# The end of a load stream: the last weight in three pieces, and a small load moved between them

## The chip, the cores and the metric

The kernel runs on one core of one Trainium2 chip. Times are device microseconds of that core, over several executions; the "span" is the part of an execution that the profile covers, from the first to the last instruction, and it is 1.8 to 2.1 us shorter than the time (that difference will matter). Ratios are the mean time of one kernel's fast runs over that of the kernel before in the same rounds, with a 95% interval, so they are not quite the ratio of the medians quoted beside them. A run is called slow when it lies over 1.5% above the fastest one of the same kernel, and fast otherwise; a single run has no known state.

## The reference, cut to what matters

One decode step of a transformer block: layer norm, attention of 8 batches with one query row over a window of 1024 cached keys, an FFN with a gate, and `x + s * g` at the end.

```python
x = A_x                                  # 8 x 1 x 512, bf16
xn = layernorm(x)
s = attention(xn, k_cache[:, :, -1024:], v_cache[:, :, -1024:], wq) @ wo   # wo: 4096 x 512
g = silu((gelu(xn @ w_gate) * (xn @ w_up)) @ w_down)                       # F = 1792
return x + s * g
```

Nearly all of the work is reading: 32 MiB of keys and values, 4 MiB each of wq and wo, 5.25 MiB of FFN weights, 47.46 MB in all (an MB is a million bytes here, an MiB 2^20).

## The kernel before

Every large load is issued by SyncE on one queue, in the order of use; the last things that it brings are `wd` (w_down) and the two halves of `wo`. The second half comes in two pieces, 12 and 4 rows of each partition. After the last piece only its matmuls, two VectorE operations and the output DMA remain. `x` is loaded twice at the very start on ScalarE's queue: as `x_sb` for the layer norm, and as `xr`, laid out for the residual at the end.

```python
nc.scalar.dma_start(out=x_sb, in_=x_flat)
xr = consts.tile([P, NW], BF16, name="xr")
nc.vector.memset(xr, 0.0)
nc.scalar.dma_start(out=xr[0:P:4, :], in_=x_flat.rearrange("b (q n) -> q b n", n=NW))

def load_rows(src, rows, r0, n, name):
    t = ring.tile([P, n, src.shape[1]], BF16, name=name, tag="slot")
    nc.sync.dma_start(out=t, in_=src.rearrange("(p r) n -> p r n", r=rows)[:, r0 : r0 + n, :])
    return t
# ... wq, then per unit the keys and values, with their matmuls (cut) ...
wd_t = load_rows(B_w_down, FJ, 0, FJ, "wd_t")
wo_t = [[load_rows(A_wo[: HT * Dh, :], WI, 0, WI, "wo_t")]]
LAST = 4
wo_t.append([
    load_rows(A_wo[HT * Dh :, :], WI, 0, WI - LAST, "wo_t"),
    load_rows(A_wo[HT * Dh :, :], WI, WI - LAST, LAST, "wo_t"),
])
# ... the FFN, and oR, the attention output laid out for wo (cut) ...
for t in range(NT):                       # the two halves of wo
    i = 0
    for w in wo_t[t]:                     # the pieces
        for r in range(w.shape[1]):       # rows: 16 in a half
            for q in range(NQ):           # 4 matmuls a row
                nc.tensor.matmul(s_ps[32*q : 32*(q+1), :], oR[:, t, i, :],
                                 w[:, r, q*NW : (q+1)*NW], ..., tile_position=(0, 32*q))
            i += 1
nc.vector.tensor_tensor(out=tmp, in0=s_ps, in1=g_sb, op=ALU.mult)
nc.vector.tensor_tensor(out=out_sb, in0=tmp, in1=xr, op=ALU.add)
nc.sync.dma_start(out=..., in_=out_sb[0:P:4, :])
```

The softmax here doesn't subtract the row's maximum and nothing guards it: scores larger than these inputs give would overflow.

## Time and profile before

| | before |
|---|---|
| time, median of 3 | 122.81 us (122.78 to 122.95) |
| span of the profiled run | 121.1 us |
| read from memory | 47.46 MB |
| share of the chain that ended last on DMA | 84% |
| last wo piece landed | 116.75 us |

First the page of the kernel before: the busy tenths of TensorE and of the DMA engines in 40 slices of the span, the granted TensorE clock in tenths, the bytes moved, and the queues (q1 is SyncE's, q10 ScalarE's, q8 brings instructions).

```profile
PE   0000799696877977979679684999969798754660
PEclk9999999999999999999999996579999955555555
DMA  4999999999999999999999999999999999999710
GB/s 100 428 435 431 411 427 419 430 422 427 419 425 425 425 425 419 427 422 425 419 430 417 433 417 430 427 419 425 422 436 438 417 417 445 428 428 415 290 68 3
q1 hardware_dynamic: 5796, 47.46, 93.3%
q8 instruction: 16, 0.26, 0.8%
q10 hardware_dynamic: 52, 0.02, 0.1%
```

The stream runs without a gap from the second slice to the 37th, at 411 to 445 GB/s, and TensorE is busy for 70% of the span. So the kernel ends when the stream ends, plus the little that follows. (The chain also has 12% of TensorE, at 74 to 87 us, since the issue of a wo load waits there for a slot that TensorE frees; loads issued earlier kept the DMA engines busy meanwhile.) Note the clock: TensorE has half of its clock in the last eight slices.

The timeline of the last stretch (start, length, engine, line, operation, tile, count; in brackets the idle time before it and what ended that) shows what follows.

```profile
111.96 1.90 PE L357 MATMUL s_ps<-wo_t,oR 128*32 128x128 bf16 x64 [1.19 <-DMA wo_t<-in_A_wo_dram]
115.60 1.90 PE L357 MATMUL s_ps<-wo_t,oR 128*32 128x128 bf16 x64 [1.74 <-DMA wo_t<-in_A_wo_dram]
117.55 0.29 DVE L365 TENSOR_TENSOR tmp<-s_ps,g_sb 128x128 f32<-128x128 f32 x1 [5.93 <-PE s_ps L357]
117.87 0.29 DVE L367 TENSOR_TENSOR out_sb<-tmp,xr 128x128 bf16<-128x128 f32 x1
118.19 0.69 SPq L368 DMA_DIRECT2D out_dram<-out_sb  x1
```

The second half of wo waits for its 12-row piece, which lands at 115.56, and then runs its 64 matmuls without another wait: when it reaches the 4-row piece, that has landed too. In the windows of the same stretch (after the engines' busy times come the clock, the DMA share, and GB/s) the DMA engines do not stop together:

```profile
113.00:113.50 0.50, 0.50 (x31) 0.50 (x24) 0.00 (x0) 0.00 (x0) 0.00 (x0) 0.50 0.91 352
113.50:114.00 0.50, 0.36 (x16) 0.17 (x5) 0.00 (x0) 0.00 (x0) 0.00 (x0) 0.50 0.54 229
114.00:115.00 1.00, 0.00 (x0) 0.00 (x0) 0.00 (x0) 0.00 (x0) 0.00 (x0) 0.50 0.45 188
115.00:116.00 1.00, 0.40 (x17) 0.40 (x20) 0.00 (x0) 0.00 (x0) 0.00 (x0) 0.50 0.43 176
116.00:116.50 0.50, 0.50 (x31) 0.50 (x24) 0.00 (x0) 0.00 (x0) 0.00 (x0) 0.50 0.13 49
```

From 113.5 to 116 us only about half of them work. The trace also records sixteen increments of a load's semaphore; for the 12-row piece the last one came at 115.56, and TensorE, which waited for that load, started at 115.60. For the last piece (4 rows) the sixteen came at

```
113.62 113.68 113.72 113.76 113.77 113.77 113.82 | 114.61 | 115.08 | 116.38 116.47 116.48 116.52 116.53 116.55 116.75
```

The increments go with engines that fall quiet: after the first seven, from 113.85 to 114.60 us, the DMA share is 0.55, or nine of the 16 engines, and 16, 9, 8 and 7 packets are under way at 113.0, 113.9, 114.7 and 115.2 us. So seven engines are done about 2.8 us before the last seven (mean against mean). TensorE did not start on the 12-row piece before its last increment, so the last seven set the kernel's end.

### The profile page before, as it was taken

What the parts mean: (1) busy time and instruction counts of PE and PEld (TensorE: products, weight loads), DVE (VectorE), ACT (ScalarE), POOL (GpSimd) and SP (SyncE); (2) the same over time, 40 slices, a digit from 0 to 9 for tenths busy, and PEclk for the clock granted to TensorE, in tenths of its full rate; (3) what the DMA queues carried; (4) which work ended last, traced back from release to release, by engine and by line L of the source; (5) the groups of instructions that cost most, each with busy time, mean ns of one, the idle gap of its engine ahead of it and who ended that gap; (6) DMA issues with size and microseconds to landing.
All of it is one profiled execution on the core that took longest, in us unless ns stands there. A gap on an engine that the chain in (4) does not pass through costs nothing.

```text
span 121.1 us, 4374 instructions
## 1 busy us (share of the span) xinstructions
PE 85.1 (70%) x2030; PEld 78.2 (65%) x2030; DVE 69.7 (58%) x145; ACT 13.3 (11%) x22; POOL 1.4 (1%) x6
## 2 busy tenths in 40 slices
PE   0000799696877977979679684999969798754660
PEld 0000799596776966869669674899868688653550
DVE  2710038685957969669678591689959400397010
ACT  3600000110110101101101010101101100100000
POOL 4000000000000000000000000000000000000000
PEclk9999999999999999999999996579999955555555
DMA  4999999999999999999999999999999999999710
GB/s 100 428 435 431 411 427 419 430 422 427 419 425 425 425 425 419 427 422 425 419 430 417 433 417 430 427 419 425 422 436 438 417 417 445 428 428 415 290 68 3
DMA packets 5865, 47.75 MB, mean 394 GB/s; under 512 B 720, under 2 KB 728, under 8 KB 856
## 3 DMA queue, kind: packets, MB, share of 16 engines
q1 hardware_dynamic: 5796, 47.46, 93.3%
q8 instruction: 16, 0.26, 0.8%
q10 hardware_dynamic: 52, 0.02, 0.1%
q14 instruction: 1, 0.01, 0.0%
HBM read 47.46 MB, written 0.01 MB: 392 GB/s over the span
## 4 chain that ended last, share of the span: by engine, by line
DMA 84%; PE 12%; DVE 0%; SPq 0%; issue 0%
DMA k_t<-in_A_k_cache_dram 51%; DMA wo_t<-in_A_wo_dram 24%; DMA wq_t<-in_A_wq_dram 10%; PE kT_ps L200 6%; PE sc_ps L217 2%; PE s_ps L357 2%; PE oT_ps L235 1%; PE sc_ps L211 1%; PE sum_ps L230 1%; SPq L93 0%; DVE tmp L365 0%; DVE out_sb L367 0%; SPq L101 0%
## 5 line engine op out<-in xcount | busy, mean ns | idle before, releaser
L204 DVE COPY kT<-kT_ps 128x1024 bf16<-128x1024 bf16 x64 | 42.9, 691 | 16.6 <-PE kT_ps L200 16.3
L200 PE MATMUL kT_ps<-ident,k_t 128*128 128x128 bf16 x512 | 41.5, 229 | 12.7 <-DMA k_t<-in_A_k_cache_dram 12.7
L200 PEld LDWEIGHTS <-k_t 128*128 128x128 bf16 x512 | 31.4, 102 | 14.0 <-DMA k_t<-in_A_k_cache_dram 13.8
L217 PE MATMUL sc_ps<-qT,kT 128*128 128x16 bf16 x512 | 22.3, 170 | 0.4 <-DVE kT L204 0.4
L217 PEld LDWEIGHTS <-kT 128*128 128x128 bf16 x512 | 20.5, 97 | 2.5 <-DVE kT L204 0.5
L224 ACT ACTIVATE pT<-sc_ps 128x512 bf16<-128x512 f32 x16 | 9.6, 597 | 80.7 <-PE sc_ps L217 80.7
L235 PEld LDWEIGHTS <-v_t 128*128 128x128 bf16 x512 | 15.4, 97 | 2.2 <-issue 0.6
L235 PE MATMUL oT_ps<-pT,v_t 128*128 128x16 bf16 x512 | 15.6, 170 | 0.0
L239 DVE TENSOR_REDUCE sums<-sum_ps 128x16 f32<-128x512 f32 x16 | 11.0, 690 | 1.1 <-PE sum_ps L230 1.1
L182 PE MATMUL qT_ps<-xnT,wq_t 128*128 128x8 bf16 x128 | 3.7, 168 | 8.1 <-DMA wq_t<-in_A_wq_dram 8.1
L182 PEld LDWEIGHTS <-wq_t 128*128 128x128 bf16 x128 | 3.6, 104 | 8.3 <-DMA wq_t<-in_A_wq_dram 8.3
L230 PE MATMUL sum_ps<-pT,ones_pp 128*128 128x512 bf16 x16 | 6.4, 403 | 0.0
L211 PE MATMUL sc_ps<-mask,ident 128*128 128x512 bf16 x16 | 6.3, 396 | 0.0
L189 DVE CAST qT<-qT_ps 128x256 bf16<-128x256 f32 x1 | 0.4, 424 | 10.0 <-PE qT_ps L182 10.0
L357 PE MATMUL s_ps<-wo_t,oR 128*32 128x128 bf16 x128 | 3.8, 311 | 2.9 <-DMA wo_t<-in_A_wo_dram 2.9
L357 PEld LDWEIGHTS <-oR 128*32 128x32 bf16 x128 | 3.4, 143 | 3.1 <-issue 3.1
L292 DVE TENSOR_SCALAR z<-z 128x112 f32<-128x112 f32 x1 | 0.2, 220 | 8.2 <-ACT z L291 8.2
L243 DVE TENSOR_TENSOR oT<-oT_ps,sums 128x16 bf16<-128x16 f32 x16 | 3.7, 229 | 2.1 <-PE kT_ps L200 0.5
L242 DVE RECIPROCAL sums<-sums 128x16 f32<-128x16 f32 x16 | 4.0, 253 | 0.5
L281 PE MATMUL gu_ps<-xnT,wu_t 128*128 128x8 bf16 x56 | 3.5, 201 | 0.7 <-DMA wu_t<-in_B_w_up_dram 0.7
L281 PE MATMUL gu_ps<-xnT,wg_t 128*128 128x8 bf16 x56 | 3.5, 201 | 0.7 <-DMA wg_t<-in_B_w_gate_dram 0.7
L281 PEld LDWEIGHTS <-wu_t 128*128 128x128 bf16 x56 | 3.4, 159 | 0.8 <-DMA wu_t<-in_B_w_up_dram 0.8
(51 smaller groups left out, 28.8 us busy)
## 6 DMA issues: line engine op xcount, KB each, us to landing
k_t<-in_A_k_cache_dram SPq DMA_DIRECT2D x16, 1024.0 KB, 20.0
v_t<-in_A_v_cache_dram SPq DMA_DIRECT2D x16, 1024.0 KB, 20.3
wq_t<-in_A_wq_dram SPq DMA_DIRECT2D x2, 2048.0 KB, 9.5
wo_t<-in_A_wo_dram SPq DMA_DIRECT2D x1, 2048.0 KB, 27.5
wg_t<-in_B_w_gate_dram SPq DMA_DIRECT2D x1, 1792.0 KB, 21.6
wu_t<-in_B_w_up_dram SPq DMA_DIRECT2D x1, 1792.0 KB, 23.4
wd_t<-in_B_w_down_dram SPq DMA_DIRECT2D x1, 1792.0 KB, 25.1
wo_t<-in_A_wo_dram SPq DMA_DIRECT2D x1, 1536.0 KB
```

Of the source, the lines that this page charges most:

```text
L182: nc.tensor.matmul(qT_ps[:, h, :], wq_t[k // 2][:, k % 2, h * Dh : (h + 1) * Dh], xnT[:, k, :], start=(k == 0), stop=(k == KD - 1),)
L200: nc.tensor.transpose(kT_ps[:, i * P : (i + 1) * P], k_t[b][:, h, t * TG + i, :], ident)
L204: nc.vector.tensor_copy(out=kT, in_=kT_ps)
L211: nc.tensor.matmul(sc[u].rearrange("p c h -> p (c h)"), ident, mask.rearrange("p c n j -> p (c n j)"), start=True, stop=False, skip_group_ ...
L217: nc.tensor.matmul(sc[u][:, t * TG + i, :], kTs[u, t][:, i * P : (i + 1) * P], qT[:, b, h * HS : (h + 1) * HS], start=False, stop=(t == NT ...
L224: nc.scalar.activation(out=pT[u], in_=sc[u], func=ACT.Exp, scale=inv_sqrt_dh)
L230: nc.tensor.matmul(sum_ps.rearrange("p c h -> p (c h)"), ones_pp, pT[u].rearrange("p c h -> p (c h)"), start=True, stop=True,)
L235: nc.tensor.matmul(oT_ps, v_t[b][:, h, c, :], pT[u][:, c, :], start=(c == 0), stop=(c == NCH - 1))
L239: nc.vector.tensor_reduce(out=sums, in_=sum_ps.rearrange("p c h -> p h c"), axis=AX.X, op=ALU.add)
L242: nc.vector.reciprocal(out=sums, in_=sums)
L281: nc.tensor.matmul(gu_ps[:, w, j, :], wt[:, k, :].rearrange("p (m j) -> p j m", j=FJ)[:, j, :], xnT[:, k, :], start=(k == 0), stop=(k == K ...
L357: nc.tensor.matmul(s_ps[32 * q : 32 * (q + 1), :], oR[:, t, i, :], w[:, r, q * NW : (q + 1) * NW], start=(t == 0 and i == 0), stop=(t == N ...
```

## The change

The intent: less work behind the last bytes (3 rows instead of 4 in the last piece), and the small load of `xr` out of the crowded start.

```diff
     x_sb = consts.tile([B, D], BF16, name="x_sb")
     nc.scalar.dma_start(out=x_sb, in_=x_flat)
     xr = consts.tile([P, NW], BF16, name="xr")
     nc.vector.memset(xr, 0.0)
-    nc.scalar.dma_start(
-        out=xr[0:P:4, :], in_=x_flat.rearrange("b (q n) -> q b n", n=NW)
-    )
...
-    LAST = 4
-    wo_t.append([
-        load_rows(A_wo[HT * Dh :, :], WI, 0, WI - LAST, "wo_t"),
-        load_rows(A_wo[HT * Dh :, :], WI, WI - LAST, LAST, "wo_t"),
-    ])
+    wo_t.append([load_rows(A_wo[HT * Dh :, :], WI, 0, 8, "wo_t")])
+
+    nc.sync.dma_start(
+        out=xr[0:P:4, :], in_=x_flat.rearrange("b (q n) -> q b n", n=NW)
+    )
+    wo_t[1].append(load_rows(A_wo[HT * Dh :, :], WI, 8, 5, "wo_t"))
+    wo_t[1].append(load_rows(A_wo[HT * Dh :, :], WI, 13, 3, "wo_t"))
```

## The prediction

> **What bounds the kernel.** The load stream. In the busy slices DMA is at 9 tenths or more from the second slice to slice 37, at 411 to 445 GB/s; 47.46 MB are read, and the chain that ended last is 84% DMA. TensorE is busy 70% of the span and is not the limit. The chain ends: the 12-row piece of the second wo half lands at 115.56 us, 64 matmuls run from 115.60 to 117.53, two VectorE operations to 118.16, then the output DMA. Its wall time is 122.81 us, 1.7 us over the span of 121.1.
>
> **How the tail is built.** The trace's semaphore landings give 16 per load, one for each DMA engine. For the 12-row piece, seven are at 112.4 to 112.6 and the last seven at 115.2 to 115.6; for the 4-row piece 113.6 to 113.8 and 116.4 to 116.75. So half of the engines end the stream about 2.7 us after the rest, and the laggards set the time. The 15 instruction-fetch packets before that (16 KB, about 0.93 us each) look like the cause: after each of the first two (18.4 and 24.4 us) one more engine lands about 1.25 us late. The change leaves TensorE's instructions, and so these, alone.
>
> On a lagging engine a row of wo takes 1.24 us / 4 = 0.31 us. Matmuls start 25 ns apart here (63 gaps in 1.6 us), and the last takes 0.31 us.
>
> **What the change does, costed.**
> 1. Pieces 8/5/3: the 8-row piece should land at about 114.3, 5 rows at 115.9, 3 rows at 116.8 (the byte order is the same). The 32 matmuls of the first piece end about 115.4, the next 20 run from 115.9 to 116.7; the last 12 wait for the landing at 116.8 and end 0.04 + 0.28 + 0.31 us later, about 117.45. Before, the 4-row piece landed at 116.75, but its matmuls were reached at 116.82, so it was nearly balanced already: the landing saves 0.07 us, four matmuls fewer behind it 0.10 us. Upper limit of the gain: about 0.17 us.
> 2. Eight more packets and one more semaphore per engine: packet starts fit 5 ns plus 37 ns per KB, so about 0.05 us lost.
> 3. xr on the stream's queue: 32 packets of 256 B on four engines (its queue shows 32 data and four semaphore packets[...]). The like-shaped output DMA spaces such packets 14 ns, so 0.11 us on four engines late, if those lag; they paid about as much early (xr landed only at 10.93 us, on ScalarE's queue)[...]. Net 0 to 0.1 us.
> 4. ScalarE loses one 0.6 us DMA issue at the start; the start waits for wq until 12.89, so nothing.
> 5. The third piece takes one more ring slot, held by a long finished k tile, and one more of 8 completion semaphores; queue depth stays many megabytes. Nothing.
>
> Sum: -0.17 + 0.05 + 0.05, about -0.07 us, all on the critical path.
>
> **Prediction:** 122.74 us, 8 in 10 between 122.45 and 123.00. Faster by over 2%: 0.005; within 2%: 0.985; slower by over 2%: 0.01.
>
> **What would show it.** Three waits of s_ps for wo in the last stretch; last landing at 116.75 to 116.95; end of s_ps 117.35 to 117.6; laggards still about 2.7 us late.
>
> **What would make it wrong.** A fetch packet moved onto a lagging engine before 116 us (it costs 0.9 to 1.25 us); small packets costing more in the stream's queue; the stream's rate itself shifting with the early start.

That the late `xr` would go to four engines was the estimate, from its four semaphore packets; the changed kernel's trace has four runs of eight packets, 14 ns apart. For point 5: the landings in the trace use eight semaphores, and when the last wo issue ended, at 89.82 us, about 11 MB were still to land (an estimate from 26.9 us to the last landing at about 0.42 MB a us).

## The result, and the profile after

| | before | after |
|---|---|---|
| time, median | 122.88 us (122.78 to 122.95, 4 runs) | 122.91 us (122.85 to 123.09, 4 runs) |
| ratio of the means of fast runs | | 1.0006, 95% interval 0.9988 to 1.0023 |
| last wo piece landed | 116.75 us | 116.86 us |
| end of s_ps on TensorE | 117.53 us | 117.44 us |

The timeline of the end, after the change:

```profile
112.03 1.90 PE L355 MATMUL s_ps<-wo_t,oR 128*32 128x128 bf16 x64 [1.12 <-DMA wo_t<-in_A_wo_dram]
114.52 1.04 PE L355 MATMUL s_ps<-wo_t,oR 128*32 128x128 bf16 x32 [0.59 <-DMA wo_t<-in_A_wo_dram]
115.97 0.73 PE L355 MATMUL s_ps<-wo_t,oR 128*32 128x128 bf16 x20 [0.41 <-DMA wo_t<-in_A_wo_dram]
116.90 0.51 PE L355 MATMUL s_ps<-wo_t,oR 128*32 128x128 bf16 x12 [0.21 <-DMA wo_t<-in_A_wo_dram]
117.46 0.29 DVE L363 TENSOR_TENSOR tmp<-s_ps,g_sb 128x128 f32<-128x128 f32 x1 [5.71 <-PE s_ps L355]
118.11 0.62 SPq L366 DMA_DIRECT2D out_dram<-out_sb  x1
```

The one wait of the second half has become three, one for each piece, and the 12 last matmuls start 0.04 us after the last landing. TensorE had been waiting 1.74 us before; now 52 of the 64 matmuls of this half are done before the last landing, but that landing is where it was, and it decides. The windows and the queues (q10 has lost the 36 packets of `xr`):

```profile
113.50:114.00 0.50, 0.42 (x16) 0.23 (x9) 0.00 (x0) 0.00 (x0) 0.00 (x0) 0.50 0.53 207
115.50:116.00 0.50, 0.09 (x8) 0.03 (x7) 0.00 (x0) 0.00 (x0) 0.00 (x0) 0.50 0.43 172
q1 hardware_dynamic: 5976, 47.47, 93.6%
q10 hardware_dynamic: 16, 0.01, 0.0%
```

The late engines are still there. The sixteen increments of the last piece (3 rows):

```
113.73 113.76 113.85 113.89 113.91 114.05 114.13 | 114.79 | 115.23 | 116.54 116.57 116.66 116.67 116.76 116.79 116.86
```

### The profile page after: what moved, and what is told of

Its sections match the earlier page's. It is cut to its first block, busy times and chain, and to the rows that moved or that the text cites. A ratio compares the mean times of both kernels' runs of the same rounds, so it can differ in the third digit from the quotient of the medians.

```text
span 121.0 us, 4362 instructions
## 1 busy us (share of the span) xinstructions
PE 85.1 (70%) x2015; PEld 78.7 (65%) x2030; DVE 69.8 (58%) x145; ACT 13.3 (11%) x22; POOL 1.4 (1%) x6
## 3 DMA queue, kind: packets, MB, share of 16 engines
HBM read 47.46 MB, written 0.01 MB: 392 GB/s over the span
## 4 chain that ended last, share of the span: by engine, by line
DMA 95%; DVE 0%; PE 0%; SPq 0%; issue 0%
DMA k_t<-in_A_k_cache_dram 51%; DMA wg_t<-in_B_w_gate_dram 18%; DMA wo_t<-in_A_wo_dram 17%; DMA wq_t<-in_A_wq_dram 10%; PE s_ps L355 0%; SPq L89 0%; DVE tmp L363 0%; DVE out_sb L365 0%; SPq L97 0%
## 5 line engine op out<-in xcount | busy, mean ns | idle before, releaser
L279 PEld LDWEIGHTS <-wg_t 128*128 128x128 bf16 x56 | 3.4, 161 | 0.9 <-DMA wg_t<-in_B_w_gate_dram 0.9
```

Of the source, the lines that this page charges most:

```text
L279: nc.tensor.matmul(gu_ps[:, w, j, :], wt[:, k, :].rearrange("p (m j) -> p j m", j=FJ)[:, j, :], xnT[:, k, :], start=(k == 0), stop=(k == K ...
```

## The experiments

Twelve runs were made. They answer five questions: what each part of the change does, whether the tail is what was summed, why half of the engines are late, whether the early ones can take over work, and where a gain in the span goes. Each expectation was written down before its run, as a theory and a rival that would show in other numbers.

### Each part alone

Pieces 8, 5 and 3, with `xr` early:

```diff
-        load_rows(A_wo[HT * Dh :, :], WI, 0, WI - LAST, "wo_t"),
-        load_rows(A_wo[HT * Dh :, :], WI, WI - LAST, LAST, "wo_t"),
+        load_rows(A_wo[HT * Dh :, :], WI, 0, 8, "wo_t"),
+        load_rows(A_wo[HT * Dh :, :], WI, 8, 5, "wo_t"),
+        load_rows(A_wo[HT * Dh :, :], WI, 13, 3, "wo_t"),
```

> Only the pieces 8, 5 and 3; x for the residual stays early on ScalarE's queue. Theory (the tail was already balanced; the last landing and the matmuls behind it decide): the last wo landing at 116.75 to 116.9 us, s_ps ends at 117.35 to 117.5 instead of 117.53, the time 0.0 to 0.15 us under before (122.88), so between 122.7 and 122.9. Rival (the pieces gain clearly, 0.2 us or more, and the late x gives it back): 122.65 or less.

Measured: 122.72 us beside 123.01, ratio 0.9983 (0.9968 to 0.9998). The last landing was at 116.89 and the time of 122.72 is in the theory's range; but the gain in the ratio, about 0.2 us, is over the theory's 0.15 and is what the rival asks for, so neither side was excluded.

`xr` late on SyncE's queue, with pieces 12 and 4:

```diff
-    nc.scalar.dma_start(out=xr[0:P:4, :], in_=...)      # at the start
...
     wo_t.append([load_rows(A_wo[HT * Dh :, :], WI, 0, WI - LAST, "wo_t")])
+    nc.sync.dma_start(out=xr[0:P:4, :], in_=...)
     wo_t[1].append(load_rows(A_wo[HT * Dh :, :], WI, WI - LAST, LAST, "wo_t"))
```

> Only x late on the stream's queue; the pieces stay 12 and 4. Theory (four of the 16 DMA engines carry its 32 packets of 256 B, 0.11 us each, and those four are among the engines that finish early): last landing within 0.1 us of 116.75, the time within 0.15 us of before, 122.75 to 123.0. Rival (small packets in the stream's own queue delay the stream's end): last landing 116.9 or later, the time 123.05 or more.

Measured: 122.88 us beside 123.01, ratio 0.9993 (0.9979 to 1.0008); last landing 116.78. Theory. The records show why it costs nothing there: in the changed kernel the 32 packets of 256 B start 14 ns apart, eight of them to an engine, 0.11 us; the four increments of `xr` came at 111.43, 111.48, 111.69 and 112.39, each shortly after one of the 8-row piece's early increments (111.25 to 111.54, and 112.21). The late engines send theirs for that piece at 114.11 to 114.48. So all four engines of `xr` are engines that have time.

Both on one chip, five rounds:

> The kernel of the first experiment once more (pieces 8, 5 and 3, x early), on one chip beside the changed kernel, because its 0.17% rests on four runs. Theory: 0.05 to 0.25 us under before. Rival (luck of that sample): ratio 0.9995 or more.

> The changed kernel itself, beside the one with x early. Theory (the late x costs next to nothing): within 0.1 us of the kernel with x early. Rival (the late x gives the gain of the pieces back): 0.15 to 0.3 us slower than that one, level with before.

Measured, with before at 122.85: `xr` early 122.77, ratio 0.9986 (0.9973 to 0.9998); `xr` late, which is the changed kernel, 122.88, ratio 0.9999 (0.9986 to 1.0011). The intervals overlap, but it is the pattern of the rival in both samples: the pieces alone are a little faster, with the late `xr` that is gone. Yet the last landings differ by less than 0.1 us, and in both directions (116.76 against 116.68 here, and 116.86 against 116.89 in the earlier runs). Part of the difference between two single profiles is the clock: in the two profiled runs with pieces of 8, 5 and 3 and `xr` early (mean granted clock 0.907 in both, against 0.870 and 0.882 in the two of the changed kernel) it went back to full in time for the last matmuls,

```profile
116.72 0.35 PE L358 MATMUL s_ps<-wo_t,oR 128*32 128x128 bf16 x12 [0.45 <-DMA wo_t<-in_A_wo_dram]
```

0.35 us for 12 matmuls, where the changed kernel needed 0.51 at half the clock. That this was chance is likely but not shown: with `xr` early and pieces of 8, 5, 2 and 1 the clock stayed at half (mean 0.876). The rest is outside the span; that comes below.

### Is the tail what was summed?

The second half of wo as one piece of 16 rows:

```diff
-    LAST = 4
-    wo_t.append([... 12 rows ..., ... 4 rows ...])
+    wo_t.append([load_rows(A_wo[HT * Dh :, :], WI, 0, WI, "wo_t")])
```

> The second half of wo in one piece of 16 rows, x early. Theory (after the last landing come n matmuls, 25 ns apart, the last 0.31 us): landing about 116.7, then 63 x 0.025 + 0.31 + 0.04 = 1.95 us, so s_ps ends at about 118.65, 1.1 us later than before: 123.9 to 124.1 us. Rival (TensorE in this tail is not what follows the landing, or runs faster when it does not wait twice): 123.4 or less.

Measured: 124.09 us beside 123.01, ratio 1.0091 (1.0076 to 1.0106), inside the theory's range.

```profile
116.93 1.90 PE L354 MATMUL s_ps<-wo_t,oR 128*32 128x128 bf16 x64 [3.06 <-DMA wo_t<-in_A_wo_dram]
```

The landing is at 116.89, and all 64 matmuls come behind it. So splitting the last load was worth 1.1 us, and the first split, into 12 and 4, had already taken nearly all of it.

The other direction, pieces of 8, 5, 2 and 1:

```diff
+        load_rows(A_wo[HT * Dh :, :], WI, 13, 2, "wo_t"),
+        load_rows(A_wo[HT * Dh :, :], WI, 15, 1, "wo_t"),
```

> Pieces of 8, 5, 2 and 1 rows, x early. Theory (behind the last landing come 25 ns per matmul at the half clock): the last landing at about 116.8 us as with 8, 5 and 3, then 4 matmuls instead of 12, so 0.2 us less, less 0.05 us for one more piece: 0.1 to 0.2 us under the version with 8, 5 and 3, which had a ratio of 0.998 and 0.999 to before; so a ratio of 0.9965 to 0.998. Rival (the pieces' gain was the clock of those runs, and more pieces cost as much as they save): a ratio of 0.999 to 1.001.

Measured: 122.71 us beside 122.92, ratio 0.9977 (0.9964 to 0.9991), in the range of the theory. The last landing was at 116.85 and the matmuls ended early:

```profile
115.96 1.23 PE L359 MATMUL s_ps<-wo_t,oR 128*32 128x128 bf16 x32 [0.50 <-DMA wo_t<-in_A_wo_dram]
```

115.96 + 1.23 = 117.19, 0.34 us before the end of s_ps in the kernel before. This version is 0.2% under before. It did not run beside the changed kernel.

### Why are half of the engines late?

The theory was that instruction fetches do it. The trace holds 4,066 TensorE records and 16 packets of 16 KB on q8, one for 254 records. Each packet that begins while the stream runs takes 0.88 to 0.97 us, on an engine that should be moving weights: beside each of the fifteen the median of data packets under way is 15, without one it is 16. Fifteen of the 16 begin before the last landing; the last one begins at 117.02. Their durations, in ns and in order of time, come back every eight packets to within 8 ns:

```
929 962 962 949 882 885 936 931 | 921 961 961 949 886 879 934
```

That is how it would look if eight engines took turns. Fifteen fetches would then be two for each of seven engines and one for the eighth, and that is the grouping of the landings above: seven late by 2.8 us, and one, at 115.08, by about 1.3.

More fetches, by 32 extra matmuls in each of 13 units (the next group overwrites what they write, so the result stays right):

```diff
+        for _ in range(32 if u < 13 else 0):
+            nc.tensor.matmul(oT_ps, v_t[b][:, h, 0, :], pT[u][:, 0, :], start=True, stop=True)
         for c in range(NCH):
```

> Before, with 416 harmless weight-load and matmul pairs more on TensorE (32 in each of 13 units; the result is overwritten by the next group, so it stays right): 832 instructions more, 3.3 instruction-fetch packets more (16 fetches now serve about 4060 instructions). TensorE has the room, 70% busy. Theory (each fetch makes one DMA engine about 1.25 us late, two rounds over the same eight engines make the 2.7 us): a third round begins, so one or more engines land about 3.9 us after the earliest ones instead of 2.7; the last landing comes 0.9 to 1.3 us later, about 117.9, the time 123.8 to 124.3. Rival (the late engines are late for another reason, such as their place in the memory): the spread of the landings stays 2.7 us, the time within 0.2 us of before.

Measured: 131.31 us, ratio 1.0704 (1.0677 to 1.073). A miss on the time: TensorE became the limit, although it had been busy for only 70%. Its page and timeline:

```profile
PE   0000999899699786999699969969896988993880
DMA  4999999999999999999999999999999999950000
q8 instruction: 19, 0.31, 0.9%
99.14 0.17 PE L235 MATMUL oT_ps<-pT,v_t 128*128 128x16 bf16 x1 [1.20 <-issue]
108.04 3.50 PE L283 MATMUL gu_ps<-xnT,wg_t 128*128 128x8 bf16 x56
```

The gate product starts at 108.04 without a wait for its weights, where before it waited for them at 96.15. By an estimate the added matmuls alone had room: 416 of about 27 ns each are 11 us, and before TensorE waited 12.7 us for keys. But the waits of this run also count 9.2 us in which TensorE is idle before a matmul and waits for nothing that the profile shows ("issue", as in the fourth line), against none in the kernel before. Seven of these gaps last 1.0 to 1.2 us, and each begins within about 0.6 us after a fetch packet's end; that TensorE then waits for instructions is likely but not shown. The landings answer the question all the same, since the stream ended while TensorE was still busy. Of 17 fetches before the last landing, each of eight engines should have two and one a third. The last piece:

```
113.50 113.56 113.63 113.64 113.69 113.78 113.95 | 114.66 | 116.42 116.42 116.44 116.59 116.66 116.69 116.70 | 118.00
```

One engine is 1.3 us behind the last of the late seven, and none is left with a single fetch's delay (115.08 before).

Fewer fetches, with matmuls left out (a wrong result; every load stays):

```diff
-        for i in range(TG):                 # scores
+        for i in range(2):
...
-        for c in range(NCH):                # values
+        for c in range(4):
...
-            for k in range(KD):             # gate and up
+            for k in range(1):
```

> Before, with work of TensorE left out: 4 of 32 matmuls in values, 2 of 8 in scores, 1 of 4 in the gate and up products. The result is wrong on purpose; all loads stay. 1832 instructions fewer, about 8 or 9 fetches instead of 16. Theory: no engine is hit twice, the last engines land about 1.3 to 1.5 us after the earliest, the last landing moves about 1.2 us forward to about 115.5, the time 121.4 to 121.9. Rival (late for another reason): spread still 2.7 us, last landing 116.75, the time 122.7 to 123.0.

Measured: 121.43 us beside 122.85, ratio 0.9883 (0.987 to 0.9897), with the same 47.46 MB read.

```profile
q8 instruction: 8, 0.13, 0.4%
113.50:114.00 0.50, 0.00 (x0) 0.00 (x0) 0.00 (x0) 0.00 (x0) 0.00 (x0) 0.50 0.58 238
115.00:116.00 1.00, 1.00 (x40) 0.78 (x32) 0.00 (x0) 0.00 (x0) 0.00 (x0) 0.50 0.00 0
114.15 1.90 PE L357 MATMUL s_ps<-wo_t,oR 128*32 128x128 bf16 x64 [1.86 <-DMA wo_t<-in_A_wo_dram]
```

The DMA engines are quiet from 115 us on, and the 12-row piece that was waited for until 115.60 is there at 114.15. The last piece:

```
113.65 113.68 113.74 113.75 113.78 113.83 113.91 | 114.75 | 114.98 114.99 115.01 115.09 115.10 115.11 115.30 115.33
```

With eight fetches, eight engines are about 1.3 us behind the early seven, all alike; with fifteen, seven of them had been 2.8 us behind and one 1.3. The early seven did not move. So the lateness comes with the fetches: 1.3 to 1.4 us for each, and the landings with 8, 15 and 17 of them fit the same eight of the sixteen engines taking turns. Why that is more than the 0.9 us of the packet itself is not known. TensorE was also less busy in this run; but the DMA engines had not run dry for it before either, and the early engines land when they did (113.65 to 113.91, before 113.62 to 113.82), so the stream did not become faster as a whole. One more engine is 0.9 to 1.0 us late in each of these runs, whatever the number of fetches. That one is open.

### Can the early engines take work from the late ones?

If so, half of 2.8 us would be to be had. The first attempt took two tiles apart by partitions, to give eight engines one partition more of each:

```diff
-    wd_t = load_rows(B_w_down, FJ, 0, FJ, "wd_t")
+    wd_t = load_split(B_w_down, FJ, 0, FJ, "wd_t", (112, 120))   # DMAs of partitions 0:112, 112:120, 120:128
-    wo_t = [[load_rows(A_wo[: HT * Dh, :], WI, 0, WI, "wo_t")]]
+    wo_t = [[load_split(A_wo[: HT * Dh, :], WI, 0, WI, "wo_t", (112, 120))]]
```

> Before, with wd and the first half of wo each loaded by three DMAs: partitions 0 to 111 (all 16 engines), then 112 to 119 and 120 to 127 (8 partitions each, so 8 engines). That moves one partition of each tile from 8 engines to the other 8: 14 KB and 16 KB at 0.0367 us per KB, 1.1 us more on one half and 1.1 us less on the other. Theory (half of the engines end 2.7 us late, and they are the ones that an 8-engine DMA does not use): the last landing comes 1.0 to 1.1 us earlier, at about 115.7, the time about 121.8. Rival 1 (the late engines are the ones that an 8-engine DMA uses): the last landing 1.1 us later, 117.9, the time about 124.0. Rival 2 (the two sets are mixed, or the lateness is no fixed set of engines): later, or no change, 122.9 to 124.0.

Measured: 136.19 us, ratio 1.1066 (1.1042 to 1.1089; one of its four runs was slow and is not in the ratio). No theory had that. The counts of packets agree with the engines that were meant: 5828 on q1 instead of 5796, 32 more, as when each tile's three DMAs end with 16, 8 and 8 semaphore packets instead of one DMA with 16. The windows of this kernel, in the middle and late (32 us):

```profile
30.00:90.00 60.00, 47.55 (x1173) 43.59 (x1171) 44.52 (x84) 7.17 (x12) 0.00 (x0) 1.00 1.01 425
92.00:124.00 32.00, 14.56 (x331) 13.11 (x327) 9.26 (x24) 1.44 (x4) 0.00 (x0) 0.58 1.01 271
```

The engines are as busy as ever and move 271 GB/s instead of 425: their packets take longer. The 16 KB packets of the first half of wo took 1160 ns (median), 611 before. A later run asks whether the partitions are the cause. The same two tiles in two DMAs each, partitions 0 to 63 and 64 to 127:

```diff
-    wd_t = load_rows(...)        # and the first half of wo
+    wd_t = load_split(B_w_down, FJ, 0, FJ, "wd_t", (64,))
```

> Before, with wd and the first half of wo loaded each by two DMAs, partitions 0 to 63 and 64 to 127[...]. It asks why the loads of 112 and 8 partitions made the time 13 us longer. Theory[...]: packets of 14 and 16 KB in these loads take about twice 535 and 611 ns, the two tiles take about 9 us longer, the time 128 to 133 us. Rival (it was the eight-engine DMAs or their number): packets at 535 and 611 ns, 122.7 to 123.3 us.

Measured, one run, its state unknown: 134.02 us, 1 us above the theory's range. (The reason of the theory and the engines that the halves were to use are cut: no run shows them.)

```profile
92.00:124.00 32.00, 14.86 (x345) 13.34 (x345) 9.10 (x23) 1.43 (x4) 0.00 (x0) 0.57 1.00 278
```

The 16 KB packets took 1207 ns, and this kernel took 11 us longer (134.02 against 122.92). So no DMA of 8 partitions is needed for it. Which engines these halves used was not read. What the two kernels share is that the tiles come in DMAs of fewer than 128 partitions; why the packets then take twice as long was not shown, nor that the cause is the same in both.

The second attempt was laid out in another way. Three rows of every partition of the second half of wo went into partitions 0 to 63 alone, by four DMAs of 32 partitions with a source of 8 by 4 blocks, meant to run on eight engines each, and on the same eight. (The contraction does not care which partition holds which row; the other operand, `oX`, was laid out alike by four small VectorE operations and six matmuls.)

```diff
+    wo_t.append([load_rows(A_wo[HT * Dh :, :], WI, 0, 8, "wo_t")])
+    for up in range(2):
+        for p0 in (0, 32):
+            nc.sync.dma_start(
+                out=wx_t[p0 : p0 + 32, up, :, :].rearrange("p r n -> p (r n)"),
+                in_=wo_rows[64 * up + p0 : 64 * up + p0 + 32, WI - NS :, :]
+                    .rearrange("(j i) r n -> i j (r n)", i=8))
+    wo_t[1].append(load_rows(A_wo[HT * Dh :, :], WI, 8, 5, "wo_t"))
```

> Rows 13 to 15 of every partition in the second half of wo come in four DMAs of 32 partitions into partitions 0 to 63 alone, in an order that gives each DMA 8 engines[...]; the rest comes in pieces of 8 and 5 rows. So eight engines carry 3 rows (24 KB, 0.92 us) more and the other eight 0.92 us less. 24 matmuls over 64 rows replace 12 over 128, and one small set of operations more prepares their operand. Theory[...]: the late group lands 0.9 us earlier, the early group 0.9 us later, last landing about 115.9 instead of 116.75, the end of s_ps about 116.7, the time 121.9 to 122.2. Rival (the late eight are a mixed set): some engines are late twice over, last landing about 117.6, the time 123.5 or more.

Its theory was that these eight would be the early engines. Measured: 123.88 us beside 122.92, ratio 1.0073 (1.0061 to 1.0085). The rival: last landing 117.75, where it had about 117.6.

```profile
116.27 0.51 PE L387 MATMUL s_ps<-wx_t,oX 64*32 64x128 bf16 x12 [0.34 <-DMA wx_t<-in_A_wo_dram]
117.79 0.73 PE L394 MATMUL s_ps<-wo_t,oR 128*32 128x128 bf16 x20 [1.02 <-DMA wo_t<-in_A_wo_dram]
```

The packets kept their length this time (16 KB in 611 ns). The first of the four DMAs has eight increments, and their times show who its eight engines were:

```
111.63 111.70 111.76 111.84 111.91 | 112.78 | 114.71 114.81
```

Five early ones, the single slow one, and two late ones. That all four DMAs use the same eight was the estimate and was not read from the trace; if they do, the two late ones carry three rows more and end the kernel: 0.92 us by the expectation's estimate, and the last landing came 1.0 us later (117.75, before 116.75).

With a finer end, pieces of 8, 3 and 2 rows beside those four DMAs:

> The same, with pieces of 8, 3 and 2 rows, so 8 matmuls instead of 20 follow the last landing. Theory (the tail after the last landing is 25 ns per matmul): 0.1 to 0.3 us under the version with 8 and 5, so 121.7 to 122.0. Rival (TensorE is then busy until the end anyway, or the smaller packets cost as much): within 0.05 us of it.

Measured: 123.48 us, ratio 1.0043 (1.0031 to 1.0055), 0.4 us under the one with 8 and 5. That is more than the 0.1 to 0.3 expected, and still slower than before. Moving work between the engines is not refuted by this; only the eight engines that these DMAs got are the wrong set.

### Where a gain in the span goes

The mean time and the mean span of each kernel's fast runs, and the number of SyncE records in the trace (one or two for each DMA that is added):

| kernel | SyncE records | time | span | time less span |
|---|---|---|---|---|
| one piece | 67 | 124.08 | 122.28 | 1.80 |
| before (beside the two below it) | 69 | 122.86 | 121.04 | 1.81 |
| pieces, xr early | 71 | 122.69 | 120.90 | 1.79 |
| the changed kernel | 73 | 122.85 | 120.82 | 2.03 |
| xr late, pieces 12 and 4 | 71 | 122.89 | 121.10 | 1.79 |
| pieces 8, 5, 2, 1, xr early | 73 | 122.71 | 120.66 | 2.05 |
| 8-engine loads, 8 and 5 | 73 | 123.84 | 121.82 | 2.03 |
| 8-engine loads, 8, 3 and 2 | 75 | 123.47 | 121.44 | 2.03 |

The last column has two values. All kernels with 67 to 71 records have 1.79 to 1.86 (also both with more and fewer fetches, at 69, and the one with halves, at 71, in one run); all with 73 or 75 have 2.01 to 2.07 (also the first attempt at moving work, at 73; spans are on record to 0.1 us, so these means are uncertain by some hundredths). Each part of the change alone brings 69 to 71; both together bring 73. The four runs of the changed kernel that were made right after the prediction had 2.07.

So the change did shorten the span, by 0.2 us (121.04 to 120.82), and 0.2 us came back outside it. That the step goes with the length of SyncE's program is a correlation over twelve kernels. The number of its DMAs alone does not fit: the kernel with halves and the changed one both issue 43, with 1.82 and 2.03 us. What happens there lies outside the profile. That cause stays open.

## Why the prediction was right

The measured time, 122.91 us, lies in the range, 0.17 us from the forecast of 122.74, and the class, within 2%, is the one given 0.985. The range, 122.45 to 123.00, also holds the kernel before, so the hit says that the change does little and does not test the sum. That the time did not move at all is in part luck: a span 0.2 us shorter, more than the forecast's 0.07, met 0.2 us outside the span that nobody had foreseen. Point by point:

- What bounds it: right. With one piece, two, three or four, the last landing stayed at 116.7 to 116.9 us, and nothing but the number of fetches moved it forward.
- Late engines through instruction fetches: a likely cause, and shown by halving the fetches (1.4 us) and by one engine's third fetch (1.3 us). The size put to it, 1.25 us, was close. "Half of the engines" was right too: seven with two fetches and one with a single one. The other engine between the groups is 0.9 to 1.0 us late with 8, 15 and 17 fetches alike; why was not shown.
- The landings at 114.3, 115.9 and 116.8 and the end of s_ps at about 117.45: 114.48, 115.93, 116.86 and 117.44.
- The limit of the gain, about 0.17 us: the end of s_ps moved by 0.09 us. One step was not in the sum: the output DMA's issue took 0.61 or 0.62 us in the three profiles with `xr` late, and 0.69 us before, also 0.07 us. The late `xr` is not needed for it: with `xr` early it took 0.68 to 0.70 us in nine profiles, but 0.61 in the two kernels with 8-engine loads. Why is not known.
- The late `xr`: "if those lag" was the open point. They do not, so it costs the last landing nothing. Landings of the same kernel differ by 0.1 us from run to run, so terms of 0.05 us, as for the eight more packets, can't be told apart here.
- What was wrong is a step that the sum took for granted: the wall time as the span and 1.7 us (the profiled run took 122.92 us, so 1.8 over its own span). In the changed kernel, with SyncE's program four records longer, it was the span and 2.03 to 2.07. That term is about 0.24 us, larger than every term that was costed, and it cancels the gain of the span. The forecast of -0.07 us came out as +0.07 us by the ratio of the first runs (1.0006) and -0.01 us by that of the later ones (0.9999), neither clear of zero.

## What to carry to other kernels

When a load stream bounds the kernel, look at the end engine by engine before cutting the last load finer: here a load was there only with its slowest engine (the last wo piece at 116.75 us, seven engines done by 113.82), and an unrolled program's own instruction fetches, not the data, made seven of the sixteen engines 2.8 us late and an eighth 1.3. Cutting the last load once took 1.1 us off, and cutting it further took a tenth or two, since behind the last landing only a few matmuls of 25 ns remain. Compare the time as well as the span: a tenth or two gained in the profile can be given back outside it, here in step with the length of the program that issues the DMAs.
